# Folding w_phi into the Q and K weights on quarters of the matmul array: a hedgehog attention and mish kernel

## Chip, cores and metric

The kernel runs on one core of one Trainium2 chip. The metric is the time of one execution on the device in microseconds, as the median of several runs. A profile is one execution recorded by the hardware profiler.

## What is computed

Two layers, each a linear attention with a learned softmax feature map ("hedgehog") and a dense block with the mish activation, both with a residual:

```python
# S = 2048, D = 640, H = 32 heads of Dh = 20, F = 1536, all float32
def A(x, wqkv, w_phi, wo):
    q, k, v = split(x @ wqkv)                               # each [H, S, Dh]
    pq = einsum("bhsd,hdf->bhsf", q, w_phi)                 # one 20x20 matrix per head
    pk = einsum("bhsd,hdf->bhsf", k, w_phi)
    phi_q = concat([softmax(pq), softmax(-pq)], -1)
    phi_k = concat([softmax(pk), softmax(-pk)], -1)
    kv, z = phi_k^T @ v, sum_s(phi_k)
    return ((phi_q @ kv) / (phi_q @ z + 1e-6)) @ wo
def B(x, w1, b1, w2):
    return mish(x @ w1 + b1) @ w2
for _ in range(2):
    x = x + A(layernorm(x), ...)
    x = x + B(layernorm(x), ...)
```

## The kernel before

All large products are made in two float32r parts: an operand is split into a high part (ScalarE copies it) and a low part (VectorE subtracts the high part), and three matmuls per tile add up high x high, high x low and low x high.

**The fold.** The kernel doesn't compute q and then q times w_phi. At the start of layer 0 it multiplies w_phi into the Q and K parts of `wqkv` once, and keeps the folded weights for both layers (they are spilled to DRAM in `wp_d` and loaded again for layer 1). A softmax doesn't change when one number is subtracted from all its inputs, so `shift_phi` (GpSimd, L255) subtracts the last of the 20 columns of each head from the others, and only DL = 19 columns per head are kept: 32 x 19 = 608 folded columns.

The operands of the fold are `bd` (w_phi as diagonal blocks) and the raw weights: `wqk_t` is wqkv transposed in DRAM, 1280 rows (Q then K) of 640 values, and `load_raw` fetches six tiles for each of Q and K. Tiles 0 to 3 hold six heads (120 rows; 128 are fetched), tiles 4 and 5 four heads (80 rows). `fold_part` makes one float32 matmul for one of the KD = 5 blocks of 128 rows of the model dimension and one tile: stationary 120 x 128 raw weights, moving 120 x 114 columns of `bd`. Three tiles (c = 0: tiles 0 to 2, 342 columns; c = 1: tiles 3 to 5, 266 columns) go side by side into one PSUM bank, and `fold_end` evicts the bank: ScalarE makes the high part (L261), VectorE the low part (L262). That is 5 x 2 banks for Q and 5 x 2 for K.

**PSUM.** There are two `mm` tiles of two banks each and four `one` tiles of one bank each. Projections use `mm` or `one` tiles, transposes of x use `one` tiles.

**The order of the work.** `attend_first` begins with a block under `written()`, in which the order on all five engines is as written. There Q is folded, the first two row tiles of x are normalised and transposed (`Transposed.step`), the first query projection `q0` is made, and the V weights are split (`make_v`). After that, for block b = 0, the order is `("q0", "v0", "v1", "k0", "q1", "k1")`, with `fold_phi` (the fold of K) just ahead of k0; from here on a planner, which simulates the engines, puts the instructions of each engine in order and may move them among the written ones. `fetch_normed(b + 1)` takes the statistics of the next block's x; for block 1 this x tile is called `early`.

Each engine works through its own list in order. All transfers are issued by SyncE (SP), in this order: x of block 0, w_phi's first half (L482), raw tiles 0 to 2 of Q, the three other pieces of w_phi (L486 to L488), raw tiles 3 to 5 of Q, five tiles of V, six raw tiles of K, `early`, and then the mask, the next x tiles and the spills to `wp_d`.

Layer 1 doesn't fold; it loads the folded weights. `attend_second` and `dense` are not touched.

Of the kernel before, what the change touches and what calls it, by code (L numbers as in the profile page):

```python
# [8 lines left out]
F32 = mybir.dt.float32  # L9
F32R = mybir.dt.float32r  # L10
AF = mybir.ActivationFunctionType
ALU = mybir.AluOpType
# [4 lines left out]
P = 128  # L17
S = 2048
D = 640
F = 1536  # L20
H = 32
DH = 20
DL = DH - 1
KD = D // P
# [7 lines left out]
QK = H * DL  # L32
# [3 lines left out]
VW = H * (DH + 1)  # L36
SKEW = 2
LAYERS = 2
LN_EPS = 1e-5
DEN_EPS = 1e-6  # L40
E_CAP = 65536.0
# [3 lines left out]
def kernel(  # L45
# [13 lines left out]
    nc = tc.nc  # L59
# [3 lines left out]
    wts = ctx.enter_context(tc.tile_pool(name="wts", bufs=1))  # L63
# [163 lines left out]
    def load_raw(which, ts=range(6)):  # L227

        raw = []
        for t in ts:  # L230
            rows = 120 if t < 4 else 80
            if t < 5:
                r = wts.tile([P, D], F32, tag=f"r2{'hl'[which]}{5 + t}", name=f"raw{which}{t}")
            else:
                r = r2_wide(10 + which, F32)[:, 0]

            n = P if t < 5 else rows
            c0 = which * D + (t * 120 if t < 5 else D - rows)
            nc.sync.dma_start(r[:n], wqk_t[c0:c0 + n, :])
            raw.append((r, rows))  # L240
        return raw

    def fold_part(ps, k, t, bd, raw):

        r, rows = raw[t]
        heads = rows // DH
        n = DL * (6 * (t % 3) if t < 5 else 10)
        nc.tensor.matmul(ps[:, n:n + heads * DL].rearrange("p (j d) -> p j d", d=DL), r[:rows, k * P:(k + 1) * P],
                         bd[:rows, t, :rows].rearrange("p (j d) -> p j d", d=DH)[:, :, :DL], start=True, stop=True)

    def shift_phi(bd, ts):

        b = bd[:, ts].rearrange("p t (j d) -> p (t j) d", d=DH) if isinstance(ts, slice) else (
            bd[:80, ts, :80].rearrange("p (j d) -> p j d", d=DH))
        nc.gpsimd.tensor_tensor(b[:, :, :DL], b[:, :, :DL], b[:, :, DL:].to_broadcast([b.shape[0], b.shape[1], DL]),  # L255
                                op=ALU.subtract)

    def fold_end(ws, ps, k, c):
        n0, n1 = (0, 18 * DL) if c == 0 else (18 * DL, QK)
        hi, lo = ws[k][0][:, n0:n1], ws[k][1][:, n0:n1]  # L260
        nc.scalar.activation(hi, ps[:, :n1 - n0], AF.Copy)  # L261
        nc.vector.tensor_tensor(lo, ps[:, :n1 - n0], hi.bitcast(F32), op=ALU.subtract)  # L262

    def fold_phi(ws, bd, raw):

        pss = {}
        for k, c in ((0, 0), (1, 0), (2, 0), (3, 0), (0, 1), (1, 1), (2, 1), (3, 1), (4, 0), (4, 1)):
            if c == 0:
                mm = None if k % 2 else mm_tile()
                pss[k] = [one_tile(), one_tile()] if k % 2 else [mm[:, 0], mm[:, 1]]  # L270
            ps = pss[k][c]
            for t in range(3 * c, 3 * c + 3):
                fold_part(ps, k, t, bd, raw)
            fold_end(ws, ps, k, c)


    def norm_stats(t, xt):
# [136 lines left out]
    def fetch(x_src, b, xt=None):  # L414
        xt = x_tile() if xt is None else xt
        nc.sync.dma_start(xt, row_block(x_src, b))
        return xt

    def attend_first(layer, x_src, first):
# [58 lines left out]
        if first is None:  # L478
            with written():
                xt = fetch(x_src, 0)  # L480
                bd = big_tile()[:120, :720].rearrange("p (t c) -> p t c", t=6)
                nc.sync.dma_start(bd[:, :3], phi_bd[:, :3])  # L482
                raw_q = load_raw(0, range(3))

                nc.vector.memset(bd[:80, 5, :80], 0.0)
                nc.sync.dma_start(bd[:40, 5, :40], phi_bd[80:120, 4, 80:120])  # L486
                nc.sync.dma_start(bd[40:80, 5, 40:80], phi_bd[:40, 5, :40])
                nc.sync.dma_start(bd[:, 3:5], phi_bd[:, 3:5])  # L488
                shift_phi(bd, slice(0, 3))
                raw_q += load_raw(0, range(3, 6))  # L490
                kv_ws = [r1_pair(k) for k in range(KD)]
                raw_v = [fetch_v(k) for k in range(KD)]
                raw = load_raw(1)
                early = fetch(x_src, 1)
                mvs = [norm_stats(t, xt) for t in range(BT)]
                norm_scale(0, mvs)
                shift_phi(bd, slice(3, 5))
                shift_phi(bd, 5)

                q_ws = [r2_pair(k) for k in range(KD)]  # L500
                mm = [mm_tile(), mm_tile()]
                pcs = [mm[0][:, 0], mm[0][:, 1], mm[1][:, 0], mm[1][:, 1], one_tile()]
                for t in range(3):
                    for k in range(KD - 1):
                        fold_part(pcs[k], k, t, bd, raw_q)
                fold_end(q_ws, pcs[0], 0, 0)
                xn = [row_tile() for _ in range(BT)]
                act(xn[0], xt[:, 0, :], AF.Identity, bias=stats[:, 0, 1, 0:1], scale=stats[:, 0, 0, 0:1])
                nc.vector.tensor_scalar(xn[1], xt[:, 1, :], stats[:, 0, 0, 1:2], stats[:, 0, 1, 1:2],
                                        op0=ALU.mult, op1=ALU.add)  # L510
                fold_end(q_ws, pcs[1], 1, 0)
                fold_end(q_ws, pcs[2], 2, 0)
                nxt = Transposed(xn)
                nxt.step()
                fold_end(q_ws, pcs[3], 3, 0)
                nxt.step()
                for t in range(3):
                    fold_part(pcs[4], 4, t, bd, raw_q)
                nxt.step()
                fold_end(q_ws, pcs[4], 4, 0)  # L520
                mm = mm_tile()
                q0 = [mm[:, 0], mm[:, 1], mm]
                project_half(q0[0], nxt, 0, q_ws, 0, 0, w=QC)

                def make_v(k):
                    split(kv_ws[k][0][:, D:2 * D], kv_ws[k][1][:, D:2 * D], raw_v[k])

                for k in range(KD):
                    ps = one_tile()
                    for t in range(3, 6):  # L530
                        fold_part(ps, k, t, bd, raw_q)
                    fold_end(q_ws, ps, k, 1)
                    if k > 0:
                        make_v(k - 1)
                project_half(q0[1], nxt, 0, q_ws, 0, 1, w=QC)
                make_v(KD - 1)
            nc.sync.dma_start(mask, bass.AP(tensor=head_mask.tensor, offset=head_mask.offset,
                                            ap=[[1, 120], [120 * (DH + 1), 3]]))
        else:
            nxt, kv_ws = first  # L540
            load_k_weights(kv_ws)
            q_ws = load_q_weights()
        for b in range(NB):
# [14 lines left out]
            for n, (kind, t) in enumerate(order):  # L558
                t = int(t)
# [335 lines left out]
    with tc.block(schedule_with_timeline_sim=True):  # L895
        src, first = x, None
        for layer in range(LAYERS):
            last = layer == LAYERS - 1
            dst = out if last else x2_d
# [39 lines left out]
            src = dst  # L939
# [38 lines left out]
```

## Time and profile before

| | |
|---|---|
| median of 3 runs | 1367.1 us (1366.75 to 1368.18) |
| the profiled execution, whole | 1366.02 us |
| its span, first to last instruction | 1364.2 us |
| granted TensorE clock | 1.000 |
| TensorE matmul (PE) busy | 1350.1 us, 99% of the span |
| VectorE (DVE) / ScalarE (ACT) / GpSimd (POOL) busy | 1057.0 / 578.2 / 472.2 us |
| DMA queue q1 | 167.22 MB, 45.9% of 16 engines' span |

How to read the lines that follow. A timeline row has the start in us, the duration in us, the engine, the line of the kernel, the operation with the tile that it writes and those that it reads, their sizes, and the number of instructions merged into the row; in brackets stands the idle time of the engine before it and what ended that. PE is the matmul stream, PEld the loading of stationary operands; a float32 matmul leaves two records in each. A tile's name is the name of the buffer that it occupies: `big` is also `bd` and the tile of V, `raw` and `r` are raw weights, `r2h` and `r2l` the parts of the folded Q weights, `r1h` and `r1l` those of K and V. A row of SPq is the issue of a transfer, not the transfer. Waits are told as "who <- what it waited for: us in total, times, longest". A window's row gives for each engine the busy time and the number of instructions, then the granted clock, the mean busy share of the sixteen DMA engines, and GB/s.

### The profile page before, as it was taken

Reading aid. Unit: us, or ns where it says so; the run is one execution under the profiler, and the core shown is the slowest. Engines: PE = TensorE matmul, PEld = TensorE weight load, DVE = VectorE, ACT = ScalarE, POOL = GpSimd, SP = SyncE. Lnnn points to the kernel's source line nnn. Section 1 sums busy time; section 2 is a strip of 40 time slices with the busy share of each in tenths; the row PEclk is TensorE's granted clock in tenths of the full one; section 3 lists DMA queues with packets and bytes.
Section 4 is the critical chain, followed back from the end, with each engine's and each line's share of the span. In section 5 each row is a group of like instructions: output and inputs, shape, how many; then the busy total and the mean of one; then the engine's idle time right before and its main releaser. Section 6 shows DMA issues by size and latency. Waiting matters only on the chain.

```text
span 1364.2 us, 30958 instructions
## 1 busy us (share of the span) xinstructions
PE 1350.1 (99%) x12896; PEld 1337.3 (98%) x12896; DVE 1057.0 (77%) x1801; ACT 578.2 (42%) x970; POOL 472.2 (35%) x422
## 2 busy tenths in 40 slices
PE   9999999999999999999999999999999999999998
PEld 8999999999999999999999999999999999999998
DVE  6888988876687887778758788779668776676775
ACT  5444344322454545445444334332235444444443
POOL 2355544444222222222246655644251211111111
PEclk9999999999999999999999999999999999999999
DMA  9533433798714442334463433558974221233200
GB/s 341 153 81 61 76 60 78 205 286 273 220 40 97 117 117 70 63 102 112 143 222 76 89 60 69 95 142 258 283 252 134 78 76 31 88 97 97 76 23 20
DMA packets 350469, 169.19 MB, mean 124 GB/s; under 512 B 287209, under 2 KB 323801, under 8 KB 350329
## 3 DMA queue, kind: packets, MB, share of 16 engines
q1 hardware_dynamic: 350329, 167.22, 45.9%
q8 instruction: 101, 1.65, 0.5%
q14 instruction: 39, 0.32, 0.1%
HBM read 104.59 MB, written 62.59 MB: 123 GB/s over the span
## 4 chain that ended last, share of the span: by engine, by line
PE 83%; DVE 3%; DMA 2%; POOL 1%; ACT 0%; issue 0%; SPq 0%; DVEq 0%; ACTq 0%; POOLq 0%
PE one L774 25%; PE mm L816 24%; PE mm L375 17%; PE one L375 11%; PE mm L652 3%; PE one L311 2%; DMA e_d<-r 1%; PE one L448 1%; DVE r L409 1%; DVE r L456 1%; DVE big L401 1%; DVE m L400 1%; DMA raw<-in_wo 0%; DMA v<-in_wv 0%; SPq L460 0%
## 5 line engine op out<-in xcount | busy, mean ns | idle before, releaser
L816 PE MATMUL mm<-r2h,ol 128*128 128x320 f32 x1280 | 304.9, 309 | 0.0
L800 POOL TENSOR_TENSOR ol<-big,ol 128x512 fp32r<-128x512 f32 (+1 forms) x98 | 130.7, 1334 | 477.8 <-ACT ol L799 419.7
L774 PE MATMUL one<-xtl,r1h 128*128 128x256 f32 x960 | 268.2, 279 | 0.0
L774 PE MATMUL one<-xth,r1l 128*128 128x256 f32 x960 | 268.0, 279 | 0.0
L774 PE MATMUL one<-xth,r1h 128*128 128x256 f32 x960 | 265.9, 279 | 0.0
L816 PEld LDWEIGHTS mm<-r2h,ol 128*128 128x128 f32 x1280 | 219.1, 188 | 0.0
L816 PE MATMUL mm<-r2l,ol 128*128 128x320 f32 x640 | 197.3, 309 | 0.0
L375 PE MATMUL mm<-r1h,xth 128*128 128x304 f32 (+1 forms) x600 | 185.2, 309 | 1.9 <-DVE r1l L262 1.5
L375 PE MATMUL mm<-r1l,xth 128*128 128x304 f32 (+1 forms) x600 | 183.9, 307 | 0.0
L375 PE MATMUL mm<-r1h,xtl 128*128 128x304 f32 (+1 forms) x600 | 183.3, 306 | 0.0
L774 PEld LDWEIGHTS one<-xtl,r1h 128*128 128x128 f32 x960 | 180.5, 188 | 0.0
L774 PEld LDWEIGHTS one<-xth,r1l 128*128 128x128 f32 x960 | 180.4, 188 | 0.0
L774 PEld LDWEIGHTS one<-xth,r1h 128*128 128x128 f32 x960 | 179.6, 188 | 0.0
L789 DVE TENSOR_SCALAR big<-big 128x512 f32<-128x512 f32 (+1 forms) x98 | 56.9, 580 | 110.3 <-ACT big L787 107.8
L816 PEld LDWEIGHTS mm<-r2l,ol 128*128 128x128 f32 x640 | 120.2, 188 | 0.0
L791 ACT ACTIVATE big<-big,two 128x512 f32<-128x512 f32 (+1 forms) x98 | 70.1, 716 | 116.9 <-DVE big L790 116.9
L787 ACT ACTIVATE big<-one,b1s 128x256 f32<-128x256 f32 x192 | 80.8, 467 | 88.3 <-PE one L774 87.8
L799 ACT ACTIVATE ol<-big 128x512 fp32r<-128x512 f32 (+1 forms) x98 | 60.9, 621 | 134.2 <-DVE big L798 134.1
L375 PEld LDWEIGHTS mm<-r1h,xth 128*128 128x128 f32 x600 | 112.8, 188 | 3.5 <-DVE r1l L262 1.7
L411 POOL TENSOR_TENSOR r<-r,r 128x1280 f32<-128x1280 f32 x32 | 77.9, 2435 | 109.1 <-DVE r L410 101.4
L375 PEld LDWEIGHTS mm<-r1l,xth 128*128 128x128 f32 x600 | 112.8, 188 | 0.2
L375 PEld LDWEIGHTS mm<-r1h,xtl 128*128 128x128 f32 x600 | 112.7, 188 | 0.0
(137 smaller groups left out, 3124.9 us busy)
## 6 DMA issues: line engine op xcount, KB each, us to landing
e_d<-r SPq DMA_DIRECT2D x128, 160.0 KB, 4.0
big<-e_d SPq DMA_DIRECT2D x32, 640.0 KB, 7.5
x_d<-xt SPq DMA_DIRECT2D x23, 640.0 KB, 4.7
xt<-x_d SPq DMA_DIRECT2D x22, 640.0 KB, 5.5
n_d<-xn SPq DMA_DIRECT2D x176, 80.0 KB, 2.2
xt<-in_x SPq DMA_DIRECT2D x16, 640.0 KB, 4.1
xn<-x_d SPq DMA_DIRECT2D x28, 320.0 KB, 4.7
v<-n_d SPq DMA_DIRECT2D x30, 256.0 KB, 3.4
```

The costliest lines, as they stand in the source:

```text
L311: nc.tensor.transpose(ps[:, c, t * P:(t + 1) * P], self.rows[t][:, (c0 + c) * P:(c0 + c + 1) * P], ident)
L375: nc.tensor.matmul(ps[:, :w], a[:, sl], r, start=(k == 0 and n == 0), stop=(k == KD - 1 and n == 2))
L400: nc.vector.tensor_reduce(m[:, s], eh[:, 1], axis=AX.X, op=op)
L411: nc.gpsimd.tensor_tensor(eg, eg, r.unsqueeze(2).to_broadcast([P, 2 * H, DH]), op=ALU.mult)
L652: nc.tensor.matmul(po[64 * q:64 * q + 64, c, GW * j:GW * j + w], phs[g][:n, s0:s0 + 64], kvb[:n, g, :w], start=True, stop=True)
L774: nc.tensor.matmul(ph[:, j, :], l, r, start=(n == 0), stop=(n == 3 * KD - 1))
L787: exps[0] = nc.scalar.activation(part(ta, 0)[:, j - js.start], ph[:, j, :], AF.Exp, bias=b1s[:, 2 * pr + j:2 * pr + j + 1]).ins
L789: nc.vector.tensor_scalar_min(e, e, E_CAP)
L791: nc.scalar.activation(r, n, AF.Ln, bias=two)
L799: nc.scalar.activation(ah[:, js], n, AF.Copy)
L800: nc.gpsimd.tensor_tensor(al[:, js], n, ah[:, js].bitcast(F32), op=ALU.subtract)
L816: nc.tensor.matmul(pys[t][:, c, :HC], l[:, j, sl], r, start=(f == 0 and n == 0), stop=(f == KF - 1 and n == 2))
```

## The change

The fold is cut into quarters of the array, and w_phi comes on another queue:

- `FOLD` lists six tiles of two groups of up to three heads. A raw tile holds the first group in partitions 0 to 63 and the second in partitions 64 to 127. Tiles 0 to 4 are still fetched by one transfer, whose source is now written as two blocks of 64 rows that overlap or lie apart; tile 5 is fetched by two transfers of 40 rows.
- `fold_part` makes four matmuls for each tile and block instead of one: for each group s (rows 64s onward) and each half q of the 128 columns. The two groups go to two PSUM banks.
- `bd` has 60 columns per tile, is set to zero first by VectorE (L485's memset covered 80 x 80), and is filled by `load_phi` with eight transfers issued by ScalarE instead of four by SP.
- `fold_end` evicts an `mm` tile's two banks in one instruction per engine, and two `one` tiles bank by bank. `pair_banks` takes either; 11 of the 20 evictions are of two `one` tiles.
- The first four blocks of Q take all four `one` tiles and both `mm` tiles; the fold of K goes block by block.

```diff
+FOLD = (((0, 3), (3, 3)), ((6, 3), (9, 3)), ((12, 3), (15, 3)), ((18, 3), (25, 3)), ((21, 3), (28, 2)), ((24, 1), (30, 2)))
...
         for t in ts:
-            rows = 120 if t < 4 else 80
+            r = (wts.tile([P, D], F32, tag=f"r2{'hl'[which]}{5 + t}", name=f"raw{which}{t}") if t < 5 else
+                 r2_wide(10 + which, F32)[:, 0])
+            (h, _), (h2, _) = FOLD[t]
+            c0 = which * D + h * DH
             if t < 5:
-                r = wts.tile([P, D], F32, tag=f"r2{'hl'[which]}{5 + t}", name=f"raw{which}{t}")
+                src = wqk_t[c0:c0 + 64, :]
+                src = bass.AP(tensor=src.tensor, offset=src.offset, ap=[[(h2 - h) * DH * D, 2]] + list(src.ap))
+                nc.sync.dma_start(r, src)
             else:
-                r = r2_wide(10 + which, F32)[:, 0]
-
-            n = P if t < 5 else rows
-            c0 = which * D + (t * 120 if t < 5 else D - rows)
-            nc.sync.dma_start(r[:n], wqk_t[c0:c0 + n, :])
-            raw.append((r, rows))
+                for s in range(2):
+                    c0 = which * D + FOLD[t][s][0] * DH
+                    nc.sync.dma_start(r[64 * s:64 * s + 2 * DH], wqk_t[c0:c0 + 2 * DH, :])
+            raw.append(r)
         return raw
 
+    def load_phi(bd):
+
+        for s in range(2):
+            nc.scalar.dma_start(bd[64 * s:64 * s + 60, :3, :60], phi_bd[60 * s:60 * s + 60, :3, 60 * s:60 * s + 60])
+        for t in range(3, 6):
+            for s, (h, n) in enumerate(FOLD[t]):
+                a, j = divmod(h, 6)
+                nc.scalar.dma_start(bd[64 * s:64 * s + DH * n, t, :DH * n],
+                                    phi_bd[DH * j:DH * (j + n), a, DH * j:DH * (j + n)])
+
     def fold_part(ps, k, t, bd, raw):
 
-        r, rows = raw[t]
-        heads = rows // DH
-        n = DL * (6 * (t % 3) if t < 5 else 10)
-        nc.tensor.matmul(ps[:, n:n + heads * DL].rearrange("p (j d) -> p j d", d=DL), r[:rows, k * P:(k + 1) * P],
-                         bd[:rows, t, :rows].rearrange("p (j d) -> p j d", d=DH)[:, :, :DL], start=True, stop=True)
+        for s, (h, heads) in enumerate(FOLD[t]):
+            n0 = DL * (3 * t if t < 3 else h - 18 - 7 * s)
+            rows = slice(64 * s, 64 * s + max(2, heads) * DH)
+            rhs = bd[rows, t, :heads * DH].rearrange("p (j d) -> p j d", d=DH)[:, :, :DL]
+            for q in range(2):
+                nc.tensor.matmul(ps[s][64 * q:64 * q + 64, n0:n0 + heads * DL].rearrange("p (j d) -> p j d", d=DL),
+                                 raw[t][rows, k * P + 64 * q:k * P + 64 * q + 64], rhs, start=True, stop=True)
...
     def fold_end(ws, ps, k, c):
-        n0, n1 = (0, 18 * DL) if c == 0 else (18 * DL, QK)
-        hi, lo = ws[k][0][:, n0:n1], ws[k][1][:, n0:n1]
-        nc.scalar.activation(hi, ps[:, :n1 - n0], AF.Copy)
-        nc.vector.tensor_tensor(lo, ps[:, :n1 - n0], hi.bitcast(F32), op=ALU.subtract)
...
+        for s in ((slice(0, 2),) if len(ps) > 2 else range(2)):
...
+            hi, lo = part(ws[k][0], s), part(ws[k][1], s)
+            nc.scalar.activation(hi, src, AF.Copy)
+            nc.vector.tensor_tensor(lo, src, hi.bitcast(F32), op=ALU.subtract)
+
+    def pair_banks(single):
+        if single:
+            return [one_tile(), one_tile()]
+        mm = mm_tile()
+        return [mm[:, 0], mm[:, 1], mm]
 
     def fold_phi(ws, bd, raw):
 
-        pss = {}
-        for k, c in ((0, 0), (1, 0), (2, 0), (3, 0), (0, 1), (1, 1), (2, 1), (3, 1), (4, 0), (4, 1)):
...
+        for k in range(KD):
+            for c in range(2):
+                ps = pair_banks((k + c) % 2)
+                for t in range(3 * c, 3 * c + 3):
+                    fold_part(ps, k, t, bd, raw)
+                fold_end(ws, ps, k, c)
...
                 xt = fetch(x_src, 0)
-                bd = big_tile()[:120, :720].rearrange("p (t c) -> p t c", t=6)
-                nc.sync.dma_start(bd[:, :3], phi_bd[:, :3])
+                bd = big_tile()[:, :360].rearrange("p (t c) -> p t c", t=6)
+                nc.vector.memset(bd, 0.0)
+                load_phi(bd)
                 raw_q = load_raw(0, range(3))
-
-                nc.vector.memset(bd[:80, 5, :80], 0.0)
-                nc.sync.dma_start(bd[:40, 5, :40], phi_bd[80:120, 4, 80:120])
-                nc.sync.dma_start(bd[40:80, 5, 40:80], phi_bd[:40, 5, :40])
-                nc.sync.dma_start(bd[:, 3:5], phi_bd[:, 3:5])
-                shift_phi(bd, slice(0, 3))
+                shift_phi(bd, 0)
                 raw_q += load_raw(0, range(3, 6))
...
-                mm = [mm_tile(), mm_tile()]
-                pcs = [mm[0][:, 0], mm[0][:, 1], mm[1][:, 0], mm[1][:, 1], one_tile()]
+                pcs = [pair_banks(k < 2) for k in range(KD - 1)]
...
+                ps = pair_banks(True)
                 for t in range(3):
-                    fold_part(pcs[4], 4, t, bd, raw_q)
+                    fold_part(ps, KD - 1, t, bd, raw_q)
...
                 for k in range(KD):
-                    ps = one_tile()
+                    ps = pair_banks(k % 2 == 0)
```

More of the change, by code (lines that the diff above doesn't have):

```diff
@@ L251, in shift_phi @@
[L251 to L256, printed above, removed]
-    def fold_end(ws, ps, k, c):
-        n0, n1 = (0, 18 * DL) if c == 0 else (18 * DL, QK)
-        hi, lo = ws[k][0][:, n0:n1], ws[k][1][:, n0:n1]
-        nc.scalar.activation(hi, ps[:, :n1 - n0], AF.Copy)
-        nc.vector.tensor_tensor(lo, ps[:, :n1 - n0], hi.bitcast(F32), op=ALU.subtract)
@@ L264, in fold_phi @@
-    def fold_phi(ws, bd, raw):
-        pss = {}
-        for k, c in ((0, 0), (1, 0), (2, 0), (3, 0), (0, 1), (1, 1), (2, 1), (3, 1), (4, 0), (4, 1)):
[L268 to L274, printed above, removed]
+                src = wqk_t[c0:c0 + 64, :]
@@ new lines, in shift_phi, with part @@
+    def shift_phi(bd, c):
+        b = bd[:, 3 * c:3 * c + 3].rearrange("p t (j d) -> p (t j) d", d=DH)
+        nc.gpsimd.tensor_tensor(b[:, :, :DL], b[:, :, :DL], b[:, :, DL:].to_broadcast([P, 9, DL]), op=ALU.subtract)
+    def fold_end(ws, ps, k, c):
+        def part(w, s):
+            if c == 0:
+                return w[:, :18 * DL].rearrange("p (t s d) -> p s t d", t=3, s=2)[:, s]
+            return w[:, 18 * DL:QK].rearrange("p (s t d) -> p s t d", s=2, t=1)[:, s]
+        for s in ((slice(0, 2),) if len(ps) > 2 else range(2)):
+            n = 9 * DL if c == 0 else 7 * DL
+            src = (ps[2][:, :, :n].rearrange("p s (t d) -> p s t d", t=3 if c == 0 else 1) if len(ps) > 2 else
+                   ps[s][:, :n].rearrange("p (t d) -> p t d", t=3 if c == 0 else 1))
+            hi, lo = part(ws[k][0], s), part(ws[k][1], s)
+            nc.scalar.activation(hi, src, AF.Copy)
+            nc.vector.tensor_tensor(lo, src, hi.bitcast(F32), op=ALU.subtract)
@@ L496, in attend_first @@
                 norm_scale(0, mvs)
-                shift_phi(bd, slice(3, 5))
-                shift_phi(bd, 5)
+                shift_phi(bd, 1)
                 q_ws = [r2_pair(k) for k in range(KD)]
-                mm = [mm_tile(), mm_tile()]
-                pcs = [mm[0][:, 0], mm[0][:, 1], mm[1][:, 0], mm[1][:, 1], one_tile()]
+                pcs = [pair_banks(k < 2) for k in range(KD - 1)]
                 for t in range(3):
@@ L516, in attend_first @@
                 nxt.step()
+                ps = pair_banks(True)
                 for t in range(3):
-                    fold_part(pcs[4], 4, t, bd, raw_q)
+                    fold_part(ps, KD - 1, t, bd, raw_q)
                 nxt.step()
-                fold_end(q_ws, pcs[4], 4, 0)
+                fold_end(q_ws, ps, KD - 1, 0)
                 mm = mm_tile()
```

## The prediction

> **What bounds the kernel now.** I read the page first, then PE's waits, then the first 60 us engine by engine, since the change touches only the start of layer 0.
>
> ```profile
> span 1364.2 us, 30958 instructions
> PE 1350.1 (99%) x12896; PEld 1337.3 (98%) x12896; DVE 1057.0 (77%) x1801; ACT 578.2 (42%) x970; POOL 472.2 (35%) x422
> ```
>
> TensorE is the bound: 1350.1 of 1364.2 us. Whatever makes it wait at the start is added to the end, and whatever takes work from it there counts only if it isn't made to wait instead. The longest such wait of the run is in the stage that is changed:
>
> ```profile
> PE mm L375 <- DVE r1l L262: 1.5, 1, 1.5
> ```
>
> In the timeline, the rows of each engine taken together:
>
> ```profile
> 30.27 0.82 PE L248 MATMUL one<-big,raw 120*128 120x114 f32 x6
> 30.92 0.83 PE L248 MATMUL mm<-big,raw 120*128 120x114 f32 x6
> ...
> 38.94 0.41 PE L375 MATMUL mm<-r1h,xth 128*128 128x304 f32 x1 [1.49 <-DVE r1l L262]
> ...
> 23.63 1.67 DVE L281 BATCH_NORM_STATS2 bn<-xt 128x6 f32<-128x320 f32 x4 [0.51 <-DMA xt<-in_x]
> ```
>
> Read it backwards. PE starts the first K projection (k0) at 38.94, when DVE has emptied a bank of folded K weights. DVE works in order, and its run of work up to there began at 23.63, when the x tile of block 1 (`early`) landed. That landing was set by the transfers (busy us and count of PE, PEld, DVE, ACT, POOL in a stretch, clock, DMA share, GB/s):
>
> ```profile
> 10.00:20.00 10.00, 9.09 (x73) 8.64 (x73) 7.39 (x15) 7.21 (x18) 0.81 (x6) 1.00 1.04 362
> 23.60:38.90 15.30, 13.45 (x105) 13.07 (x103) 12.63 (x34) 8.81 (x19) 6.38 (x8) 1.00 1.00 382
> 42.00:60.00 18.00, 18.00 (x130) 18.00 (x130) 13.61 (x19) 5.88 (x9) 3.19 (x3) 1.00 0.48 109
> ```
>
> All sixteen DMA engines are full (share 1.04 and 1.00) until the stage is over; from 42 us PE is busy all of its time (18.00 of 18.00). So the stage is a queue of transfers, then a chain on DVE, then PE without gaps. From 23.63 to 38.94 DVE has 12.63 us of work in 15.3 us.
>
> The order of the queue, from SP's timeline, and the one wait that shows its depth:
>
> ```profile
> 0.72 0.39 SPq L416 DMA_DIRECT2D xt<-in_x  x1
> 1.17 0.47 SPq L482 DMA_DIRECT2D big<-in_phi_bd  x1
> 1.69 1.34 SPq L239 DMA_DIRECT2D raw<-in_wqk_t  x3
> 3.07 0.36 SPq L486 DMA_DIRECT2D big<-in_phi_bd  x1
> 3.48 0.33 SPq L487 DMA_DIRECT2D big<-in_phi_bd  x1
> 3.85 0.33 SPq L488 DMA_DIRECT2D big<-in_phi_bd  x1
> 5.17 0.91 SPq L239 DMA_DIRECT2D raw<-in_wqk_t  x2
> ...
> 10.70 3.53 SPq L239 DMA_DIRECT2D raw<-in_wqk_t  x5
> 14.73 0.33 SPq L239 DMA_DIRECT2D r<-in_wqk_t  x1
> 15.56 0.33 SPq L416 DMA_DIRECT2D xt<-in_x  x1
> ```
>
> ```profile
> SPq L239 <- DMA xt<-in_x: 1.0, 1, 1.0
> ```
>
> SP issues eight transfers and holds the ninth until the first has landed (5.17). The five large raw tiles of Q, those of V and K all stand ahead of `early` (15.56).
>
> **Part 1: how a raw tile is fetched. This decides.** Ten tiles of 128 rows (five of Q, five of K) are still one transfer each, but the source was one run of 128 rows and is now written as two blocks of 64 rows, `[[.., 2], [D, 64], [1, D]]`, 60 or 140 rows apart, against 128 partitions. What the trace gives is the rate:
>
> ```profile
> raw<-in_wqk_t SPq DMA_DIRECT2D x10, 320.0 KB, 6.3
> big<-in_phi_bd SPq DMA_DIRECT2D x1, 168.8 KB, 4.5
> big<-in_phi_bd SPq DMA_DIRECT2D x1, 112.5 KB, 5.7
> ...
> GB/s 0 154 396 329 369 325 319 285 386 396 401 394 400 256 323 353 403 410 403 403 401 393 291 380 370 375 381 191 148 241 135 149 309 253 57 14 0 0 0 0
> ```
>
> (The GB/s are slices of 1.5 us.) At the sustained 403 GB/s a tile of 327,680 bytes takes 0.81 us, and one engine of the sixteen moves 25.2 GB/s. The fast end: the new transfer is dealt over sixteen engines as now, 0.81 us, no change. The slow end: it is dealt out by the outermost count that source and destination share, which is two, and two engines carry 163,840 bytes each: 163,840 / 25.2 = 6.5 us. Every other transfer of this kernel has 32 rows or more outermost on both sides, so no row tells the ends apart. I take the slow end: a list of two blocks against 128 rows must be cut anew before sixteen engines can share it evenly, and nothing in the code cuts it.
>
> By the Trainium skill, page "DMA: Bandwidth & Descriptors", section "Why a DMA increments its semaphore by 16 and not by 1", a transfer runs on the largest number of engines up to 16 that divides the slowest dimension of both sides; 128 against 2 gives 2, and that rule puts the sum at the slow end too. No run here shows it yet.
>
> The same two engines also have their share of every other transfer, so everything queued behind waits for them. Ten tiles cost 10 x (6.5 - 0.81) = 57 us more ahead of `early`. W_phi's 168.8 and 112.5 KB leave the queue (-0.7 us at 403 GB/s). The eight w_phi transfers stand before the raw tiles in the program; if the depth of eight holds for both queues together, the first raw tile waits for the first w_phi piece to land (0 to +2 us: that piece can't be issued before 2.0, below, and 4.5 is how long its forerunner took). Together +56 to +59; `early` lands at about 23.63 + 57 = 80.6.
>
> From there the chain is as it was: statistics, normalisation, features of q0, evictions of K, k0. DVE's 12.63 us at best, the present 15.3 us at worst: k0 starts at 93.2 to 95.9; I take 94, **+55 us**. What else is late is covered: PE reaches the folds of K at 30.27 with q0, v0 and v1 done; these need Q's five tiles, so +28.5, which is 59 and ahead of 80. After k0 the queue is 57 us late and PE 55, the same relation as now, so I add nothing.
>
> **Part 2: the fold itself.** A fold of three tiles is 6 records (a float32 matmul leaves two) in 0.65 us (30.27 to 30.92), 20 such groups, 13 us. It becomes 24 records on quarters of the array. No row has quarters; the nearest are halves and column strips:
>
> ```profile
> 330.00 1.38 PE L652 MATMUL mm<-kvb,big 120*64 120x63 f32 x40
> 331.21 0.27 PE L652 MATMUL mm<-kvb,ol 80*64 80x42 f32 x4
> 331.30 1.36 PE L652 MATMUL mm<-kvb,big 120*64 120x63 f32 x40
> ...
> 65.01 0.83 PE L448 MATMUL one<-big,v 128*21 128x40 f32 x64
> 65.78 0.33 PE L311 MATMUL one<-ident,xn 128*128 128x128 f32 x1
> ```
>
> Halves of 64 columns start every 1300 / 44 = 29.5 ns, strips every 770 / 64 = 12 ns. So a group costs 24 x 29.5 = 0.71 (rows don't overlap, +1 us in all) down to 24 x 12 = 0.29 (-7 us); I take half of 29.5, since two halves of the rows double the two halves of the columns: 0.36, -6 us of PE work. The Trainium skill, "TensorE: Matmul & The Clock Gate", section "Wait — 56ns, not 53.3ns?", says that starts never come closer than 25 ns, by which a group would cost 0.6 us; the row of 12 ns speaks against it. All this work lies ahead of k0, where PE waits anyway, so I count it at nothing; without that cover DVE's 12.63 us after 23.63 would allow k0 at 36.3, at most -2.7.
>
> Eleven of the 20 pieces are evicted bank by bank, so ACT and DVE get eleven more instructions each.
>
> ```profile
> 0.71 1.28 ACT L60 ACT_TABLE_LOAD   x1 [0.71 <-PEq L969]
> 9.67 0.46 ACT L261 ACTIVATE r2h<-mm 128x342 fp32r<-128x342 f32 x1 [7.67 <-PE mm L248]
> 32.29 0.44 ACT L261 ACTIVATE r1h<-one 128x342 fp32r<-128x342 f32 x1
> 33.30 0.41 ACT L261 ACTIVATE r1h<-mm 128x266 fp32r<-128x266 f32 x1
> ```
>
> 76 columns fewer save 0.03 us on ACT, so a split costs 0.1 to 0.35; five fall among K's evictions, 0.5 to 1.8 us on the chain; that lies within the 2.7 us between its two ends above.
>
> **Part 3: w_phi.** ACT issues eight transfers once its table is there (0.71 + 1.28 = 2.0), 0.33 to 0.47 us each by SP's rows, done near 5.5, before its first work at 9.67: hidden. A ninth would queue behind x's landing, and nothing on ACT would wait for that. The memset grows from 80 to 360 columns on a DVE that is idle until x lands, and POOL's shift covers half the columns; both lie beside the wait for raw tiles. The first folds of Q hold all four `one` banks, so the transposes wait for two evictions, 1 us at most, and that too is before 59.
>
> **The sum** is made against the profiled execution, 1366.0 us (span 1364.2 and 1.8 around it), 1.1 below the median of 1367.1: 1366.0 + 55 = **1421**.
>
> **Rivals.**
> *K's weights alone set k0 (0.15).* The planner orders DVE anew; if `early` isn't ahead of K's evictions, k0 waits only for K's last tile. Issued at 14.73, and 6.3 us to landing as the raw tiles' row has it, it is there at 21, then 78; five folds of 0.36 and an eviction of some 0.9 (ACT's 0.41 and about as much on DVE) follow, k0 near 81: +42, 1408. Against it: x of block 1 is fetched and its statistics taken before q0's features in the program, and so in DVE's rows.
> *The transfer is dealt over sixteen engines after all (0.15), so the change of source does nothing.* Then the queue is as long as now and the fold decides. PE loses 6 us of work ahead of k0 and DVE's chain from 23.63 allows 2.7 us: 1363.3, **faster**. It decides the other way where the five more evictions (0.5 to 1.8) and the columns without overlap take that back: 1365 to 1368. For it: PE waits 1.49 us at k0 on DVE, so PE's gain isn't the whole; against: that same wait.
> *The two engines are slower than a full sixteen's share (0.1 of the first case).* At the 362 GB/s of 10 to 20 us an engine gives 22.6, a tile takes 7.2 us, +64, 1429.
>
> **The numbers.** About 0.2%, 2.7 us, is what can be told from no change. Two engines and DVE's chain 0.70, two engines and K's weights 0.15, sixteen engines 0.15, of which faster 0.05, within 0.2% 0.07, slower 0.03. So faster 0.05, same 0.07, slower 0.88. Range 1404 to 1430: the second case less 4 us for a faster rate and a shorter chain, up to the slower engines; it leaves out the sixteen-engine case and some 0.04 beyond.
>
> **What would show it.** Right: raw tiles landing 6 to 7 us apart, GB/s near 50 from 5 to 75 us, PE idle for some 50 us before 95, DVE's statistics of `early` waiting for `DMA xt` until about 80, PE gapless after k0. Wrong: raw tiles still 0.8 us apart in the first 20 us, or L248's records starting 30 ns apart in a stage that PE bounds; or statistics of `early` taken after K's evictions, which is the second case.

## Result and profile after

The changed kernel takes 1441.43 us (median of four runs, 1440.66 to 1442.34); the kernel before, on the same chip, 1367.16 (1366.75 to 1368.18). The ratio is 1.0547 [1.0535, 1.0559]: 74.3 us slower, where 55 were predicted, and above the range.

The page's head and PE's waits of the changed kernel:

```profile
span 1438.7 us, 31703 instructions
PE 1355.5 (94%) x13256; PEld 1342.2 (93%) x13256; DVE 1059.4 (74%) x1812; ACT 579.8 (40%) x981; POOL 472.1 (33%) x421
...
PE mm L264 <- DVE r2l L285: 44.9, 1, 44.9
PE one L264 <- DMA raw<-in_wqk_t: 16.1, 3, 5.4
PE mm L264 <- DVE r1l L285: 5.3, 2, 3.7
PE one L264 <- issue: 4.8, 1, 4.8
```

The span grew by 74.5 us and PE's busy time by only 5.4, so 69 us are PE standing still. The largest wait is not for a transfer but for DVE: 44.9 us, once, for the low part of a folded Q weight (`r2l`).

The raw tiles and `early`, in the timelines of SP, PE and DVE, and the rate (GB/s, slices of 3.25 us from 0 to 130):

```profile
1.16 20.24 SPq L239 DMA_DIRECT2D raw<-in_wqk_t  x5
68.01 0.35 SPq L442 DMA_DIRECT2D xt<-in_x  x1
...
18.59 0.69 PE L264 MATMUL one<-big,raw 60*64 60x57 f32 x16 [5.34 <-DMA raw<-in_wqk_t]
25.02 0.70 PE L264 MATMUL one<-big,raw 60*64 60x57 f32 x16 [5.30 <-DMA raw<-in_wqk_t]
...
31.13 0.57 DVE L285 TENSOR_TENSOR r2l<-one,r2h 128x171 fp32r<-128x171 f32 x2
81.20 1.67 DVE L307 BATCH_NORM_STATS2 bn<-xt 128x6 f32<-128x320 f32 x4 [49.51 <-DMA xt<-in_x]
...
GB/s 115 148 52 53 51 52 57 52 78 73 135 52 280 150 50 52 50 52 50 50 55 234 238 147 134 32 207 355 310 3 165 90 195 237 64 131 304 319 74 5
```

A window of the time in which only raw tiles of K are under way, laid out as in the prediction:

```profile
50.00:60.00 10.00, 0.00 (x0) 0.00 (x0) 0.00 (x0) 0.00 (x0) 0.00 (x0) 0.50 0.13 51
```

This is the prediction's first step as it stood: tiles land 6.4 us apart, the rate sits at 50 to 52 GB/s, and `early` is there at 81.2 (predicted 80.6). The window says more than the rate can: the sixteen DMA engines are busy for a share of 0.13, which is two of sixteen (0.125). Counted packet by packet in the trace, two packets are under way at a time for 93% of these 10 us; in the kernel before, from 20 to 25 us, sixteen or more are, all of the time. So two engines are full and fourteen stand. But DVE's two rows show what it didn't have: at 31.7 DVE is through with the first half of Q and its next instruction is the statistics of `early`. It stands there for 49.5 us. What comes behind them, in the same view, and what PE, ACT and SP do meanwhile:

```profile
84.61 0.48 DVE L285 TENSOR_TENSOR r2l<-one,r2h 128x133 fp32r<-128x133 f32 x2
89.86 0.81 DVE L142 TENSOR_TENSOR r1l<-big,r1h 128x640 fp32r<-128x640 f32 x1
102.00 1.67 DVE L307 BATCH_NORM_STATS2 bn<-xt 128x6 f32<-128x320 f32 x4 [5.38 <-DMA xt<-in_x]
105.09 0.46 DVE L285 TENSOR_TENSOR r1l<-mm,r1h 128x342 fp32r<-128x342 f32 x1
...
85.70 0.68 PE L264 MATMUL mm<-big,raw 60*64 60x57 f32 x16 [44.90 <-DVE r2l L285]
100.33 0.57 PE L264 MATMUL mm<-big,raw 60*64 60x57 f32 x24
100.72 0.40 PE L264 MATMUL one<-big,raw 60*64 60x57 f32 x16
105.61 0.91 PE L264 MATMUL mm<-big,raw 60*64 60x57 f32 x24 [3.67 <-DVE r1l L285]
113.40 0.60 PE L401 MATMUL mm<-r1h,xth 128*128 128x304 f32 x1
...
96.37 1.73 ACT L133 ACTIVATE xn<-xt,stats 128x640 f32<-128x640 f32 x2
...
98.12 0.33 SPq L442 DMA_DIRECT2D xt<-in_x  x1
```

DVE's evictions of Q's second part (`r2l`) and its splits of V (`r1l<-big` is the last) all come after 81.2. PE had done its folds into every free bank by 40.8; it goes on at 85.70. q0's second half, v0 and v1, which the prediction had done by 59, run from 85 to 100. A second wait of the same kind follows: the x of block 3 goes into the buffer that `early` holds (x has two), ScalarE has read `early` out of it at 98.10 (96.37 + 1.73), SP issues the transfer at 98.12, it lands at 102.0, and its statistics stand ahead of K's evictions (`r1l`, 105.09). So k0 starts at 113.40 and not at 94: 74.5 us later than before, which is the span's difference. Of these, 57.6 us lie ahead of `early` (81.20 against 23.63) and 16.9 between `early` and k0 (32.2 against 15.3).

In the kernel before, DVE's list had the other order: Q's second part, V's splits and one bank of K (22.62), and only then `early`, whose row at 23.63 stands in the prediction.

```profile
16.61 0.43 DVE L262 TENSOR_TENSOR r2l<-one,r2h 128x266 fp32r<-128x266 f32 x1 [1.69 <-ACT r2h L261]
...
21.88 0.82 DVE L141 TENSOR_TENSOR r1l<-big,r1h 128x640 fp32r<-128x640 f32 x1
```

### The profile page after: what moved, and what is told of

The parts are those of the page before. It is cut to its first block, busy times and chain, and to the rows that moved or that the text cites. A ratio compares the mean times of both kernels' runs of the same rounds, so it can differ in the third digit from the quotient of the medians.

```text
span 1438.7 us, 31703 instructions
## 1 busy us (share of the span) xinstructions
PE 1355.5 (94%) x13256; PEld 1342.2 (93%) x13256; DVE 1059.4 (74%) x1812; ACT 579.8 (40%) x981; POOL 472.1 (33%) x421
## 4 chain that ended last, share of the span: by engine, by line
PE 88%; DMA 4%; SPq 3%; DVE 3%; POOL 1%; issue 1%; ACT 0%; DVEq 0%; POOLq 0%; ACTq 0%
PE mm L401 25%; PE one L795 23%; PE mm L837 23%; PE one L401 11%; PE mm L673 3%; SPq L239 2%; PE one L337 2%; DMA raw<-in_wqk_t 2%; PE one L474 1%; DMA xt<-in_x 1%; DVE r L482 1%; DMA v<-in_wv 0%; DVE r L435 0%; SPq L243 0%; DMA raw<-in_wo 0%
## 5 line engine op out<-in xcount | busy, mean ns | idle before, releaser
L437 POOL TENSOR_TENSOR r<-r,r 128x1280 f32<-128x1280 f32 x32 | 78.0, 2437 | 98.9 <-DVE r L436 72.7
```

Source lines behind the costliest of these rows:

```text
L437: nc.gpsimd.tensor_tensor(eg, eg, r.unsqueeze(2).to_broadcast([P, 2 * H, DH]), op=ALU.mult)
```

## Experiments

The theory after this: about 57 us come from the two-block source (two DMA engines), about 19 from DVE's new order, in which statistics of an x that is still on its way stand ahead of evictions that PE waits for. The main rival: the fold in quarters costs the 19 us itself. All times are medians; "before" was measured beside each group of four on the same chip (1365.78 for the first four, 1366.37 for the next four, 1366.49 for the last four), and times of different groups are compared by their distance to it.

| experiment | us | ratio to before | minus before |
|---|---|---|---|
| e1: before, raw tiles as two blocks | 1423.49 | 1.0419 [1.0399, 1.0438] | +57.7 |
| e2: changed, statistics held behind V's splits | 1432.85 | 1.0488 [1.0468, 1.0508] | +67.1 |
| e3: changed, two transfers per raw tile | 1386.30 | 1.0147 [1.013, 1.0163] | +20.5 |
| e4: changed, raw tiles consecutive in DRAM | 1384.87 | 1.0136 [1.0121, 1.0151] | +19.1 |
| e5: changed, statistics held, block 3's too | 1422.84 | 1.0415 [1.0401, 1.0429] | +56.5 |
| e6: e4 and e5 together | 1369.85 | 1.0029 [1.0017, 1.0042] | +3.5 |
| e7: before, statistics of `early` first | 1380.52 | 1.0104 [1.009, 1.0117] | +14.2 |
| e8: before, raw tiles as four blocks | 1394.23 | 1.0207 [1.0191, 1.0223] | +27.9 |
| e9: before, w_phi on ScalarE's queue | 1366.50 | 1.0000 [0.9991, 1.0009] | 0.0 |
| e10: e6 with w_phi on SP | 1369.88 | 1.0026 [1.0016, 1.0037] | +3.4 |
| e11: e10 with K's folds earlier | 1369.78 | 1.0028 [1.0016, 1.0039] | +3.3 |
| e12: changed, PE kept busy while it waits | 1439.23 | 1.0536 [1.052, 1.0552] | +72.7 |

**e1, the source alone.** The kernel before; only the form of the source changes (row 64 of a tile then holds row 60 of the weights).

```diff
-            nc.sync.dma_start(r[:n], wqk_t[c0:c0 + n, :])
+            src = wqk_t[c0:c0 + n, :]
+            if t < 5:
+                src = bass.AP(tensor=src.tensor, offset=src.offset, ap=[[60 * D, 2], [D, 64], [1, D]])
+            nc.sync.dma_start(r[:n], src)
```

> The kernel before, with one change: each of the ten large raw tiles is still one transfer, but its source is written as two blocks of 64 rows, 60 rows apart (the second block is read four rows early, so the folded weights are made of other rows; nothing else differs). VectorE's order is the old one: the statistics of early stand behind the V splits. Theory 1 (the transfer runs on two engines, and the rest of the loss comes from the order on VectorE): raw tiles 6.5 us apart, early near 81 us, k0 near 94, total 1421 (1415 to 1427), that is what the prediction's chain gives. Rival 2 (two engines, but the loss beyond 55 us comes from elsewhere, the clock or the spills): 1435 or more. Rival 3 (the source's form costs nothing): 1367.

Measured: 1423.49, +57.7. Its DVE and PE timelines:

```profile
80.10 1.67 DVE L284 BATCH_NORM_STATS2 bn<-xt 128x6 f32<-128x320 f32 x4 [14.51 <-DMA xt<-in_x]
...
95.41 0.41 PE L378 MATMUL mm<-r1h,xth 128*128 128x304 f32 x1
```

This is the prediction's chain within 2.5 us (80.6, then 93.2 to 95.9, of which it took 94, then 1421), and the order on DVE is the old one. DVE waits 14.5 us for `early` here, not 49.5, since all that it could do before that is done. The prediction priced this kernel, not the changed one.

**e2, the order on DVE, first try.** The changed kernel; the statistics of blocks 1 to 3 may not be issued before the last split of V.

```diff
+            if b <= 3:
+                with tc.issue_after(last_split[0]):
+                    norm_scale(b, [norm_stats(t, xt) for t in range(BT)])
```

> The changed kernel, with one change: on VectorE the statistics of the x tiles of blocks 1 to 3 are held behind the last split of V, so the evictions of Q's second part no longer stand behind the landing of early. Transfers are as in the changed kernel. Theory 1 (the 20 us beyond the prediction are q0's second half, v0 and v1 that VectorE's order held back until early had landed): PE makes them between 38 and 60 us, k0 near 95, total 1421 to 1428. Rival 2 (the clock, or Q's spills in SP's queue ahead of block 3's x tile): 1435 to 1441, no change.

Measured: 1432.85, between the two cases expected and only 7 us nearer to its before than the changed kernel (67.1 against 74.3). The 44.9 us wait is gone, another has grown. PE's waits, and DVE's timeline:

```profile
PE mm L265 <- DVE r1l L286: 10.2, 2, 8.8
...
92.87 1.67 DVE L308 BATCH_NORM_STATS2 bn<-xt 128x6 f32<-128x320 f32 x4 [5.17 <-DMA xt<-in_x]
```

The x of block 3 still stands ahead of K's evictions, and PE waits for these 10.2 us in all. e5 takes that up.

**e3 and e4, the transfers made fast.** The changed kernel, with each large raw tile fetched by two transfers of 64 rows (e3), or by one transfer of 128 rows that lie one after another, the rows having been laid out so in DRAM (e4).

```diff
+                for s in range(2):                                   # e3
+                    c0 = which * D + FOLD[t][s][0] * DH
+                    nc.sync.dma_start(r[64 * s:64 * s + 64], wqk_t[c0:c0 + 64, :])
...
+                nc.sync.dma_start(r, wqk_t[c0:c0 + P, :])            # e4
```

> The changed kernel, with each of the ten large raw tiles fetched by two transfers of 64 rows instead of one of two blocks. Theory 1 (the form of the source is the whole loss): raw tiles 0.8 us apart, GB/s near 390 from 4 us on, total 1363 to 1368; the fold in quarters takes 0.37 us a group instead of 0.65 and gives at most 2.7 us. Rival (the fold in quarters, or w_phi on the other queue, costs something of its own): 1370 or more.

> The changed kernel, with the raw rows laid out in DRAM in the order of the tiles, so that each large tile is one transfer of 128 consecutive rows; the rest is as in the changed kernel. Theory 1: as the kernel before or a little better, 1362 to 1367, and not slower than with two transfers each, since SP issues ten transfers fewer and eight in flight hold twice the bytes. Rival (the fold in quarters costs something of its own): 1370 or more.

Measured: 1386.30 and 1384.87. The first case of each expectation missed by 18 us and the rival's 1370 or more came: with the two-block source gone, the kernel is still 19 to 21 us slower. In e4, PE's waits, and DVE's and PE's timelines:

```profile
PE mm L261 <- DVE r2l L282: 12.5, 1, 12.5
PE mm L261 <- DVE r1l L282: 5.3, 2, 3.6
...
25.08 1.67 DVE L304 BATCH_NORM_STATS2 bn<-xt 128x6 f32<-128x320 f32 x4 [9.95 <-DMA xt<-in_x]
...
57.40 0.60 PE L398 MATMUL mm<-r1h,xth 128*128 128x304 f32 x1
```

These are the two waits of the changed kernel, the first shorter (12.5 for 44.9), the second the same (5.3): `early` lands at 25, nearly as before, and DVE stands 10 us for it, with Q's evictions behind. From `early` to k0 it is 32.3 us, as in the changed kernel (32.2). So 19 us don't come from the two-block source; it costs the other 55 (74.3 against 19.1; 57.7 in e1). Whether the 19 are the order's or the fold's, e4 doesn't say.

The transfers of e3 aren't as fast as those of e4. DVE's timeline of e3:

```profile
30.43 0.89 DVE L307 BATCH_NORM_STATS2 bn<-xt 128x6 f32<-128x320 f32 x2 [8.81 <-DMA xt<-in_x]
```

`early` lands 5.4 us later than in e4. That the times agree within 1.4 us comes from another order: in e3 the planner put two of DVE's rows of Q's second part (20.70 and 21.19) ahead of `early`, in e4 none.

**e5 and e6, the whole hold.** As e2, and the statistics of block 3 behind the last eviction of K's folded weights as well; e6 is the same edit in e4.

```diff
+                with tc.issue_after((last_split if b < 3 else last_fold)[0]):
```

> The changed kernel, with the statistics of blocks 1 and 2 written on DVE behind the last split of V, and those of block 3 behind the last eviction of K's folded weights. Theory (DVE's order: the statistics of a late x stand ahead of evictions that PE waits for): the 19 us go and the 57 us of the ten raw tiles stay, 1421 to 1426, with k0 near 94 and no wait of PE on the lo parts of K over 3 us. Rival (the fold in quarters itself, with its eleven more evictions and its wider columns, costs those 19 us in whatever order): 1433 to 1441, with DVE busy where PE waits.

> The same hold in the kernel whose large raw tiles lie as 128 consecutive rows in DRAM, each one transfer over sixteen engines (1384.9 without the hold). Theory (order): the whole loss goes, 1363 to 1367 beside 1365.8 for the kernel before, and PE's waits come back to 10 us or less in all. Rival (the fold in quarters costs it): 1380 to 1386. Between the two: what the hold doesn't reach, such as block 3's x behind the spills on SP's queue, 1368 to 1378.

Measured: 1422.84, as expected, and 1369.85, between the two cases. Each against its before, e5 is within 1.2 us of e1 (56.5 and 57.7); the order accounts for 18 us of the 74.3, and in e4 for 15.6 of the 19.1. The fold in quarters, which is in both kernels unchanged, doesn't cost them: the rival falls, but for the 3.5 us left in e6. With the hold ScalarE also reads `early` sooner, and x of block 3 is issued at 86.32 instead of 98.12. k0 in e5, in PE's timeline, where the prediction had 94:

```profile
96.43 0.61 PE L402 MATMUL mm<-r1h,xth 128*128 128x304 f32 x1
```

e6 is left 3.5 us above the kernel before. Its windows, PE first, the clock before the last two columns:

```profile
5.00:10.00 5.00, 2.85 (x108) 2.52 (x106) 1.81 (x8) 0.27 (x2) 1.79 (x7) 1.00 0.98 322
10.00:15.00 5.00, 3.94 (x43) 3.46 (x40) 3.90 (x10) 3.70 (x11) 0.47 (x1) 0.66 0.87 290
...
30.00:35.00 5.00, 2.91 (x136) 2.60 (x137) 3.59 (x9) 3.00 (x9) 1.52 (x2) 1.00 1.03 402
35.00:40.00 5.00, 3.74 (x120) 3.45 (x116) 3.81 (x10) 2.76 (x9) 2.36 (x1) 0.51 0.94 347
```

PE, with a cheaper fold, waits more (2.85 and 2.91 of 5 us busy, where the kernel before has 4.54 and 4.60), and after each such stretch the granted clock falls, to 0.66 and 0.51. The first product of features and V (`one<-big,v`) starts at 68.82 instead of 65.01, 3.8 us late. This profiled execution lies 2.5 us above e6's median and its span is 6.1 us longer than before, so it lost another 2.3 us later; that all of the median's 3.5 us lie in this stage is not shown.

**e7, the order alone.** The kernel before, its fold and transfers untouched; only the statistics of `early` are written ahead of Q's second part (and the planner then put some of K's evictions ahead of it too).

```diff
+                norm_scale(1, [norm_stats(t, early) for t in range(BT)])
                 mm = mm_tile()
                 q0 = [mm[:, 0], mm[:, 1], mm]
```

> The kernel before, its own fold and transfers, with the statistics of block 1 written ahead of the evictions of Q's second part. Theory (order): DVE waits for early's landing at 23.6 with Q's second part behind it, and the kernel loses some of the 19 us although neither fold nor transfers change: 1372 to 1386. Rival (the order alone is harmless, since early lands at 23.6 already): 1365 to 1368.

Measured: 1380.52, +14.2. DVE's timeline:

```profile
23.58 0.89 DVE L281 BATCH_NORM_STATS2 bn<-xt 128x6 f32<-128x320 f32 x2 [3.08 <-DMA xt<-in_x]
...
28.06 0.77 DVE L262 TENSOR_TENSOR r2l<-one,r2h 128x266 fp32r<-128x266 f32 x2
```

The same eviction that stood at 16.61 before comes at 28.06. An order alone makes the kernel 1% slower, with no operation changed: the theory's cause works without the change. (The x of block 3 stands ahead of K's evictions here too: DVE waits 6.29 us for it at 47.05.)

**e8, four blocks.** The kernel before, each large raw tile written as four blocks of 32 rows.

```diff
+                src = bass.AP(tensor=src.tensor, offset=src.offset, ap=[[31 * D, 4], [D, 32], [1, D]])
```

> The kernel before, each large raw tile written as four blocks of 32 rows, 31 rows apart (so the folded weights hold other rows than the reference's, and the output with them). Theory (as many engines as the outermost count): four engines, 327680 / (4 x 25.2) = 3.25 us a tile instead of 0.81, ten tiles +24, 1388 to 1392, and early lands near 48. Rival (only the gap between blocks, or the hand-written source as such, sends a tile to two engines): 1421 to 1424 or 1366.

Measured: 1394.23, +27.9. `early` in DVE's timeline, and a window of raw tiles alone:

```profile
50.29 1.68 DVE L284 BATCH_NORM_STATS2 bn<-xt 128x6 f32<-128x320 f32 x4 [7.53 <-DMA xt<-in_x]
...
30.00:35.00 5.00, 0.77 (x2) 0.50 (x2) 1.39 (x3) 0.19 (x1) 0.00 (x0) 0.68 0.26 102
```

The busy share is 0.26, four of sixteen (0.25), at twice the 51 GB/s of two blocks, and four packets are under way at a time for 87% of the window. `early` is there 26.7 us later than before, or 0.81 + 2.67 = 3.5 us a tile where four engines at 25.2 GB/s would need 3.25. Between two blocks (+56.5 for `early` in e1) and four the cost halves: the outermost count sets it. The time is 2 us above the expected span.

**e9 and e10, w_phi's queue.** e9 is the kernel before with its four w_phi transfers on ScalarE; e10 is e6 with the eight on SP.

```diff
-                nc.sync.dma_start(bd[:, :3], phi_bd[:, :3])
+                nc.scalar.dma_start(bd[:, :3], phi_bd[:, :3])
```

> The kernel before with its four w_phi transfers issued by ScalarE, and nothing else changed; DVE's order of instructions stays as it was. Theory (w_phi on ScalarE's queue is hidden, as the prediction said): 1365 to 1367, within 0.2% of before. Rival (it lands later beside the raw tiles, and PE's first fold waits for the shift of w_phi on POOL, as a wait of 2.2 us in the kernel with 128 consecutive rows and the hold suggests): the first fold moves from 6.6 to about 8.4 us and the time to 1367.5 to 1369.5.

> The kernel with 128 consecutive rows for each large raw tile and the hold (1369.85), with w_phi's eight transfers on SP ahead of the raw tiles. Theory (w_phi's queue): at most 2 of the 3.5 us left come back, 1367 to 1368.5, with PE's wait for POOL gone. Rival (eight issues of 0.33 to 0.47 us on SP put off the raw tiles by 2 us and the x tile with them, so the wait only changes its name): 1369 to 1371. What is left in both is K's evictions on DVE behind the features of q0.

Measured: 1366.50 and 1369.88. The queue costs nothing in the kernel before. In e6, PE waits 2.2 us at the first fold for POOL's shift of w_phi; in e10, in PE's waits, that one has only got another name, as its rival said:

```profile
PE one L262 <- DMA raw<-in_wqk_t: 1.9, 1, 1.9
```

**e11, K's folds ahead of v1.** e10 with one number changed, meant to give DVE time for K's evictions.

```diff
-                if b == 0 and n == (1 if layer else 3):
+                if b == 0 and n == (1 if layer else 2):
```

> The same kernel as the one with w_phi on SP, and the folds of K written behind v0 (position 2 of block 0) instead of behind v1 (position 3), so that PE has v1 to do while DVE empties K's banks. Theory (what is left is PE waiting at k0 for K's evictions): 3 to 5 us less, 1362 to 1365, the first of these kernels at or below the kernel before. Rival (PE reaches the folds before K's raw tiles have landed at about 22, or the loss is elsewhere): 1366 to 1370.

Measured: 1369.78, as its rival had it. PE's waits:

```profile
PE mm L262 <- DVE r1l L283: 5.4, 1, 5.4
```

PE reaches K's folds 5 us sooner and waits there for DVE, which has the statistics of `early` and the features of q0 first: what was gained in front is waited for behind. The best that the quartered fold reached here is the level of e6, e10 and e11, 0.3% above the kernel before.

**e12, the clock.** The changed kernel; PE makes 300 transposes of the identity into an unused bank while it has nothing to do.

```diff
+                    if k == 3:
+                        for _ in range(300):
+                            nc.tensor.transpose(q0[1][:, :P], ident, ident)
```

> The changed kernel with 300 transposes of the identity into an unused bank (some 40 us of PE work at full clock) where PE stands from 40.4 to 85.7, so that the clock stays up. Theory (after 81 us the chain is DVE's, and PE's half clock in it costs only what DVE waits for): 3 to 5 us less, 1436 to 1439. Rival (the half clock is what makes the folds and the projections of 85 to 113 late): 8 to 14 us less, 1427 to 1433. If neither counts: 1440 to 1443.

Measured: 1439.23, 2.2 less and between the expected cases; the intervals of the two ratios overlap. One of its PE waits, rows of its DVE and PE timelines, and a window of e12, then the same window of the changed kernel:

```profile
PE mm L264 <- DVE r2l L285: 8.6, 1, 8.6
...
79.45 1.67 DVE L307 BATCH_NORM_STATS2 bn<-xt 128x6 f32<-128x320 f32 x4 [48.29 <-DMA xt<-in_x]
...
103.41 0.91 PE L264 MATMUL mm<-big,raw 60*64 60x57 f32 x24 [3.68 <-DVE r1l L285]
...
80.00:90.00 10.00, 6.06 (x69) 5.98 (x70) 8.93 (x28) 2.61 (x6) 2.94 (x8) 0.55 0.60 212
```

```profile
80.00:90.00 10.00, 4.30 (x59) 4.22 (x60) 8.79 (x29) 2.61 (x6) 2.77 (x7) 0.50 0.49 183
```

`early` happens to land 1.75 us sooner, and the wait at K's folds ends 2.2 us sooner (103.41 against 105.61). But the experiment doesn't do what it was meant to: the transposes end 8.6 us before PE can go on at 83.94, the clock falls again, and from 80 to 90 us it is 0.55, where the changed kernel has 0.50. So what a full clock would be worth in this stretch is not shown.

## Why the prediction failed

**Part 1 was right in rule and size.** Two blocks outermost put a transfer on two engines: `early` at 81.20 for 80.6, +57.7 in e1 for +55 to +57, and a busy share of 0.13 of sixteen engines. The rule that the prediction cited, of the Trainium skill's page "DMA: Bandwidth & Descriptors", section "Why a DMA increments its semaphore by 16 and not by 1", agrees with these runs: two, and with four blocks (e8) four engines.

**The step that failed is the one behind it: "From there the chain is as it was" and "What else is late is covered".** The prediction counted 15.3 us at most from `early` to k0, as in the kernel before. The rows show when `early` is there and when k0 starts:

| kernel | `early`, us | k0, us | between |
|---|---|---|---|
| before | 23.63 | 38.94 | 15.3 |
| e1: before, two blocks | 80.10 | 95.41 | 15.3 |
| changed | 81.20 | 113.40 | 32.2 |
| e4: changed, fast transfers | 25.08 | 57.40 | 32.3 |
| e5: changed, statistics held | 80.11 | 96.43 | 16.3 |

The prediction took for granted that q0, v0 and v1 would be done by 59, because in the trace of before DVE had made what they need (Q's second part, V's splits) ahead of `early`. That was DVE's order, not a dependence. The prediction named the planner only as something that could put `early` behind K's evictions; it didn't ask what would happen if the planner put `early` further ahead. Then everything behind it on DVE is as late as it is, with 57 us of delay here. This cost 18 us (74.3 above before against 56.5 in e5): the first hold gave back 7 (e2), taking the x of block 3 from ahead of K's evictions 11 more (e5). With 18 more the prediction's 1421 would have been 1439.

Why the planner prefers this order wasn't tested on its own. The two-block source alone (e1) and w_phi's queue alone (e9) leave the old order; e4, with fast transfers, has the new one. So it comes with the rest of the change (the fold in quarters with its banks and evictions, the eight pieces of w_phi, the larger memset), and which of these it is stays open.

The signs that the prediction named for being right (tiles 6 to 7 us apart, 50 GB/s, DVE waiting for `early` until about 80) all came: they tested part 1 and not the step behind it.

**Part 2 had the rate right; that it is worth nothing holds only in part.** 24 records of a group take 0.39 us (100.33 to 100.72 above) for 0.36 predicted, 16 ns each; in the trace they start in sets of four, 6 to 7 ns apart within a set, a set every 58 ns. The page "TensorE: Matmul & The Clock Gate" of the Trainium skill, section "Wait — 56ns, not 53.3ns?", by whose 25 ns a group is estimated at 0.6, doesn't hold for these quarters at full clock. At the half clock, 105.61 to 106.29 and on, a group takes 0.65 to 0.69. "Counted at nothing" left out that a fold which is made behind a wait of PE is made at half clock, and the question whether a changed fold changes the planner's order.

**Part 3** (w_phi hidden) holds for the queue itself (e9), though ScalarE's eight issues took until 9.97 us in the changed kernel and not 5.5. With the eight pieces, the first fold starts at 8.42 us in e6 and at 8.22 in e10, by either queue, and at 6.59 in the kernel before; that was not in the sum.

**The rivals.** K's weights alone: no, in the changed kernel `early` (81.20) stands ahead of all of DVE's evictions of K (the first at 105.09). Sixteen engines: no; and where sixteen engines are given (e4, e6), the time is +19 or +3.5, not -3 to +2, so that rival was too cheap as well: of its "PE loses 6 us of work" nothing is left in e6, where PE is busy for 60.25 us ahead of the first product of features and V, and for 60.40 in the kernel before.

## What to carry to other kernels

When a transfer is made late, list for each engine what stands behind the first instruction that needs it; an engine that works in order is late with all of it, whether or not that work depends on the transfer. If the order comes from a planner, an edit of one stage can reorder another, so an order read from the trace of before is an assumption to be priced, not a fact. A transfer's source should have its many rows outermost: two blocks of 64 rows in one transfer took 6.4 us a tile, two transfers of 64 rows (e3) brought `early` at 30.4, one run of 128 (e4) at 25.1.

## What the runs showed of the hardware

In the changed kernel the granted clock falls to 0.50 once PE has stood for a few microseconds, and stays there for some microseconds of work. Four of its windows:

```profile
5.00:10.00 5.00, 2.32 (x15) 2.08 (x13) 1.86 (x6) 0.00 (x0) 1.30 (x4) 0.99 0.18 57
10.00:15.00 5.00, 1.12 (x32) 0.97 (x32) 0.23 (x2) 0.00 (x0) 0.96 (x5) 0.50 0.14 53
...
25.00:30.00 5.00, 4.21 (x67) 3.60 (x67) 3.47 (x9) 3.53 (x9) 0.00 (x0) 0.50 0.24 82
30.00:35.00 5.00, 2.78 (x25) 2.46 (x23) 1.31 (x4) 0.80 (x3) 0.00 (x0) 0.96 0.32 107
```

PE stands from 7.3 to 12.1 us and the clock is a half; from 25 to 30 PE is busy 4.21 of 5 us and the clock still a half; then it is back. A group of the fold takes 0.65 to 0.69 us there for 0.39, which fits that PE's busy time rose by 5.4 us although the fold is cheaper, and that e6, whose fold should save some 5 us at full clock (an estimate: 20 groups, 0.39 for 0.65), doesn't show it.

ScalarE's transfers are issued while its table is being loaded; the prediction let them wait for it. ScalarE's timeline of the changed kernel:

```profile
0.71 1.28 ACT L61 ACT_TABLE_LOAD   x1 [0.71 <-PEq L990]
1.31 1.02 ACTq L250 DMA_DIRECT2D big<-in_phi_bd  x2
```
